# One attention stage, re-planned: merged value copies, a quarter of x moved by transfers, separate input loads

## The chip, the cores and the metric

The kernel runs on one core of a Trainium2 chip. The metric is the device time of the whole kernel in microseconds, the median of several runs. Engines are named as in the profile: PE is TensorE (matmuls), ACT is ScalarE, DVE is VectorE, POOL is GpSimd, SP is SyncE, which here only issues transfers.

## The reference

A gated linear attention over 4 batches, 8 heads, 768 steps and 48 features, and behind it a mixture of 8 experts whose gates are balanced over all tokens:

```python
f = 1.0 / (1.0 + np.exp(-f_logit))
for t in range(S):
    state = f[:, :, t, :, None] * state + np.einsum('bhd,bhe->bhde', k[:, :, t], v[:, :, t])
    y[:, :, t] = np.einsum('bhd,bhde->bhe', q[:, :, t], state)
...
logits = x @ w_gate                      # x: y as (3072, 384)
P = np.exp(logits - logits.max())
for _ in range(8):
    P /= P.sum(1, keepdims=True) + 1e-09
    P /= P.sum(0, keepdims=True) + 1e-09
    P *= N / E
for e in range(E):
    out += P[:, e:e + 1] * (np.maximum(x @ w1[e], 0.0) @ w2[e])
```

## The kernel before

Every number is kept as two 16-bit halves, a high and a low part, and a product is three matmuls. The high part is made by ScalarE (a copy with conversion), the low part by VectorE (value times scale minus high part).

The attention is cut into 24 items of 128 tokens (`attend(i)`). Three items are a unit `u` (384 tokens of a half batch), two units are a batch `b`. An item has streams of steps, each named by a letter: L loads its inputs; K makes the decayed keys (exponential, logarithm, a scan on VectorE, high and low keys, a transposing transfer); d the decays; Q the queries; V the values; A the scores; S the running states; c the carried state; Y the outputs, which end as the parts `xh` and `xl` of x; g the gates' logits. The first three items turn their keys on TensorE (T, U) instead of by transfers.

The output of an item lies in PSUM as four blocks of 96 rows. Three blocks go to rows 0 to 95 of x in one instruction; the fourth is cut into three pieces of 32 rows that go to rows 96 to 127, one instruction each (`PCS`, lines 642 and 648 by way of the helpers). So an item has four copies on ScalarE and four on VectorE. The values are rounded once to a compact high and low part (`vhc`, `vlc`) and written once more, for each of two heads and both parts, to block diagonal tiles (`vh`, `vl`): four copies of 64 x 384, for the first three items two of them by GpSimd.

While the attention runs, TensorE is filled with the first two experts' products over tokens that are ready ("filler", `raw_pairs`, streams named F; one F is one matmul). Filler results leave PSUM by evictions: E on ScalarE, D on VectorE. The second product of a filler pair is stored to memory (`put`, line 491) and added later. Filler uses a ring of four PSUM banks (`bank`). The gates' small product uses 16 spare columns of the bank of the keys-values product (`spare`, `kv_bank`).

The order in which every engine's instructions are issued is written out in `PLAN`: each word takes one step of a stream, `F3` takes three filler matmuls, `W25` 25 idle warm-up matmuls, `B` a step of the balancing of the gates (`balance`), `C0` to `C3` a step of `convert(b)`, which prepares the tokens of a batch for the paired products, `k0` to `k3` the preparation of the first weights. `X` stands behind the last gates: there the attention's memory is given back. All transfers named here are issued from SP's queue, in order.

Behind the plan comes the paired stage: for the other experts, products of blocks in a scheme that needs fewer multiplications (`period`, `paired`, tiles `kb_*`, `kyps`, `kxps`). It begins with one matmul into each of five PSUM banks (`kb_touch*`).

Of the kernel before, what the change touches and what calls it, by code (L numbers as in the profile page):

```python
# [9 lines left out]
F32 = mybir.dt.float32  # L10
# [9 lines left out]
NP = H // 2  # L20
# [34 lines left out]
A_IN_PSUM = range(3, 24)  # L55
LOW_BY_DVE = (0, 1, 2)
VL_BY_POOL = (0, 1, 2)
# [3 lines left out]
G L0 a0 a1 a2 a3 B a4 a5 a6 a7 L1 z G K0 W25 K0 Z K0 K0 Z Z Z K0 V0 K0 z a0 V0 K0 d0 K0 K0 V0 T0 K0 Q0 U0 W1 a0 T0 T0 U0 U0 W3 Q0 T0 b0 U0 L2 S0 Q0 c0  # L61
d0 V0 V0 S0 W3 Q0 a1 V0 c0 S0 A0 a1 S0 a2 W8 A0 a3 b1 S0 A0 S0 a2 a4 Y0 Y0 A0 a5 a3 Y0 a6 Y0 Y0 Y0 a4 Y0 Y0 Y0 a5 Y0 F1 b2 F1 K1 F6 K1 F2 Y0 F2 b3 a7
Y0 Y0 Y0 F1 K1 F1 K1 V1 g0 F5 b0 F9 g0 F1 a6 F2 d1 F1 K1 F10 E F3 K1 F6 Q1 F5 D F4 K1 F7 Q1 F3 K1 F4 K1 F1 E F1 L3 T1 U1 K1 Q1 F3 T1 D F1 Q1 F2 U1 F1
a7 F1 d1 T1 K2 F2 S1 A1 T1 K2 F1 V1 F2 V1 F2 V1 F1 A1 V1 S1 V2 K2 V1 F1 A1 F3 K2 b1 Y1 S1 A1 S1 Y1 E K2 U1 d2 K3 Y1 K2 U1 S1 V2 c1 S1 S1 Q2 S1 Y1 Y1
K2 c1 Y1 Q2 K2 K2 Y1 L4 T2 Y1 U2 K2 Y1 Y1 F2 Q2 Y1 F6 T2 T2 Q2 Y1 F3 Y1 F1 U2 Y1 F1 U2 b0 F1 T2 g1 F5 U2 F1 A2 d2 V2 S2 F2 g1 F2 V2 F1 A2 F1 S2 b2 V2
b1 c2 V2 A2 F6 b3 F3 S2 Y2 A2 F1 S2 F1 Y2 F1 E F9 K3 F6 Y2 K4 D F9 S2 F1 c2 F5 b2 F1 S2 F5 E F1 Y2 S2 Y2 V3 F1 D F1 K4 F3 S2 V4 F3 b3 F3 Y2 F1 K3 K3
F1 Y2 F2 Y2 F1 Y2 F1 Y2 F2 Y2 F1 K3 d3 F2 Y2 F4 Y2 E F4 Y2 F3 d3 K3 F2 Q3 F3 S3 F5 g2 V3 F1 K3 F9 K3 F3 K3 F3 g2 F1 K4 F3 E F9 V3 F7 K3 F1 V3 F7 V3 F8
V3 F5 D F3 E F8 V4 F1 K4 F2 K4 F1 K3 F1 d4 F6 D F1 V4 F7 d4 F1 K4 E F3 V4 F1 D F2 K4 F2 Q3 F1 K4 F1 K4 F2 L5 V4 F3 V4 F2 K4 F1 Q3 F4 Q3 S3 E F1 K4 F1
S3 S3 Q4 F2 S3 F3 A3 c3 S3 Q4 S4 S3 F5 A3 F2 Q4 L6 F9 S3 F2 A3 F6 S3 F3 K5 F3 A3 F2 E Y3 F1 Q4 F1 K5 Y3 F1 D V5 F1 Y3 F1 K5 K5 A4 Y3 F1 K6 F1 A4 d5 Y3
F1 Q5 F1 V5 Y3 F1 E F3 Q5 F4 Y3 F7 Y3 F3 Y3 F3 Y3 Y3 F3 A4 F5 Y3 F3 Q5 F1 Y3 F3 Y3 F2 A4 E F3 d5 g3 K5 D Y4 F2 V5 Y4 g3 K5 F1 V5 F1 Y4 Q5 S4 K5 F1 S4  # L70
S4 K5 K5 F1 S4 F2 V5 F2 E F2 K5 F1 V5 F1 c4 F1 S4 F3 S4 F1 S4 F4 S5 F1 E F1 K5 F2 L7 F3 K6 F2 S4 A5 V6 Y4 A5 F4 Y4 F3 K6 K6 F1 Y4 A5 F6 Y4 F7 Y4 F2 A5
F1 Y4 F2 d6 F2 E F6 V6 F2 Y4 F3 K6 F3 D F7 d6 F2 Q6 F2 Y4 F8 K7 F1 Y4 F3 Y4 F4 Y4 F1 E F2 K6 F7 V6 F3 g4 D Y5 K6 F4 Y5 g4 Q6 K6 F2 K6 F2 Y5 S5 V6 F2
# [91 lines left out]
DH = DM // 2  # L164
# [1319 lines left out]
```

## Time and profile before

| what | us |
|---|---|
| median of 3 runs | 1490.27 (1488.26 to 1490.68) |
| the profiled execution, its own time | 1490.65 |
| its span, first to last instruction | 1488.8 |
| TensorE, ScalarE, VectorE, GpSimd busy in it | 1444.7, 1167.7, 1274.0, 1060.1 |

The span leaves out 1.85 us around the instructions. Matmuls are pipelined and their ends are modelled, so a high busy time of TensorE alone doesn't show that it sets the pace; a count of matmuls times the beat at which they start does.

### The profile page before, as it was taken

To read this page: it belongs to the slowest core of one execution; us is meant where nothing else is said; L and a number is where in the kernel's file an instruction comes from. 1 tells how busy PE (TensorE), PEld (TensorE's weight loads), DVE (VectorE), ACT (ScalarE), POOL (GpSimd) and SP (SyncE) were. 2 spreads that over 40 slices of the span, in tenths; PEclk is the share of its full clock that TensorE was granted. 3 is DMA by queue.
4 is the path that set the end of the run, shared out by engine and by line. 5 is a ranking of instruction groups with operands and counts; after the bars stand their busy time and mean duration, and the time that the engine had idled before them with its cause. 6 is when DMAs were issued, how large, how long until landed. Compare 5 with 4: busy or idle time off the path is not lost.

```text
span 1488.8 us, 40831 instructions
## 1 busy us (share of the span) xinstructions
PE 1444.7 (97%) x16125; PEld 1276.8 (86%) x16125; DVE 1274.0 (86%) x2585; ACT 1167.7 (78%) x2636; POOL 1060.1 (71%) x1259
## 2 busy tenths in 40 slices
PE   7988999999999999999999999999999999999997
PEld 5777766666679999999999999999999999999997
DVE  7878979988869989999988888888888898888876
ACT  8888998874467788888888888887777777778764
POOL 3233443338436699999999999998888888888763
PEclk9999999999999999999999999999999999999999
DMA  8435545520200122221121111110000000000012
GB/s 261 112 102 131 136 116 142 126 48 33 77 31 12 29 61 60 56 60 49 49 60 50 40 53 50 55 49 23 23 23 23 22 23 20 15 13 23 2 55 78
DMA packets 82234, 88.97 MB, mean 60 GB/s; under 512 B 49808, under 2 KB 69392, under 8 KB 82032
## 3 DMA queue, kind: packets, MB, share of 16 engines
q1 hardware_dynamic: 81600, 85.68, 20.9%
q8 instruction: 128, 2.10, 0.6%
q14 instruction: 74, 0.61, 0.1%
q10 hardware_dynamic: 432, 0.59, 0.1%
HBM read 62.46 MB, written 14.16 MB: 51 GB/s over the span
## 4 chain that ended last, share of the span: by engine, by line
PE 78%; ACT 9%; DVE 7%; DMA 4%; issue 2%; SPq 0%; ACTq 0%; DVEq 0%
PE kyps L374 30%; PE kb_A L374 9%; PE kb_B L374 9%; PE kb_D L374 7%; PE kxps L374 5%; PE kb_C L374 5%; PE yps L374 4%; PE hps L374 4%; DMA q<-in_qkf_dram 3%; PE kb_E L374 2%; PE kb_F L374 2%; ACT xh L642 1%; DVE xl L648 1%; DVE sl L648 1%; ACT kb L642 1%
## 5 line engine op out<-in xcount | busy, mean ns | idle before, releaser
L374 PEld LDWEIGHTS <-k1h 128*128 128x128 f16 x3120 | 293.6, 98 | 22.0 <-issue 2.1
L374 PE MATMUL kyps<-k2h,kgh 128*128 128x192 f16 x1248 | 307.2, 246 | 1.5 <-ACT kyps L1189 1.5
L374 PE MATMUL kyps<-k2h,kgl 128*128 128x192 f16 x1248 | 307.4, 246 | 0.0
L374 PE MATMUL kyps<-k2l,kgh 128*128 128x192 f16 x1248 | 307.3, 246 | 0.0
L374 PEld LDWEIGHTS <-kgh 128*128 128x128 f16 x2496 | 229.8, 98 | 8.8 <-issue 1.8
L1359 POOL TENSOR_TENSOR kgl<-kf,kgh 128x512 f16<-128x512 f32 x153 | 204.2, 1335 | 4.4 <-ACT kgh L1356 4.4
L1192 DVE SCALAR_TENSOR_TENSOR yy<-kyps,pes,part 128x192 f32<-128x192 f32 x282 | 117.0, 415 | 102.4 <-PE kyps L374 92.2
L1231 POOL TENSOR_TENSOR acc<-acc,yy 128x384 f32<-128x384 f32 x141 | 141.0, 1000 | 67.0 <-DVE yy L1192 67.0
L1359 POOL TENSOR_TENSOR kgl<-kr,kgh 128x512 f16<-128x512 f32 x153 | 181.1, 1184 | 9.8 <-PE kyps L374 8.3
L374 PEld LDWEIGHTS <-k1l 128*128 128x128 f16 x1560 | 152.6, 98 | 17.7
L374 PEld LDWEIGHTS <-kh 128*128 128x128 f16 x1248 | 117.2, 98 | 8.7 <-issue 1.8
L374 PEld LDWEIGHTS <-kgl 128*128 128x128 f16 x1248 | 122.1, 98 | 0.1
L1189 ACT ACTIVATE kyps<-kyps 128x192 f32<-128x192 f32 x156 | 50.1, 321 | 73.4 <-PE kyps L374 71.3
L1336 POOL TENSOR_TENSOR kr<-kr 128x256 f32<-128x256 f32 x104 | 78.8, 758 | 38.8 <-ACT kr L1325 36.4
L1310 ACT ACTIVATE cp<-kb_A 128x512 f32<-128x512 f32 x156 | 93.3, 598 | 16.6 <-DVE kb_A L1312 15.5
L1356 ACT ACTIVATE kgh<-kf 128x512 f16<-128x512 f32 x156 | 98.6, 632 | 0.4 <-DVE kf L1333 0.4
L1356 ACT ACTIVATE kgh<-kr 128x512 f16<-128x512 f32 x156 | 97.9, 628 | 0.0
L645 POOL TENSOR_TENSOR kb<-q,kb 48x512 f16<-48x512 f32 x42 | 54.3, 1294 | 61.0 <-ACT kb L642 47.8
L374 PEld LDWEIGHTS <-w1h 128*128 128x128 f16 x1008 | 74.2, 100 | 24.1 <-issue 3.1
L374 PE MATMUL yps<-w2h,hh 128*128 128x384 f16 x288 | 94.7, 329 | 0.0
L374 PE MATMUL yps<-w2l,hh 128*128 128x384 f16 x288 | 94.7, 329 | 0.0
L374 PE MATMUL yps<-w2h,hl 128*128 128x384 f16 x288 | 94.6, 329 | 0.0
(285 smaller groups left out, 5484.1 us busy)
## 6 DMA issues: line engine op xcount, KB each, us to landing
q<-in_qkf_dram SPq DMA_DIRECT2D x23, 672.0 KB, 5.7
k1r<-in_w_dram SPq DMA_DIRECT2D x26, 384.0 KB, 3.0
k2r<-in_w_dram SPq DMA_DIRECT2D x26, 384.0 KB, 3.1
ys<-yr SPq DMA_DIRECT2D x48, 192.0 KB, 2.0
yb<-ys SPq DMA_DIRECT2D x48, 192.0 KB, 2.4
vr<-in_vbd_dram SPq DMA_DIRECT2D x24, 192.0 KB, 4.5
out_dram<-acc SPq DMA_DIRECT2D x21, 192.0 KB, 1.9
w1r<-in_w_dram SPq DMA_DIRECT2D x6, 384.0 KB, 7.2
```

The lines of the kernel that those rows point to most:

```text
L374: ins = (nc.tensor.transpose if transpose else nc.tensor.matmul)(**kw)
L642: pin(nc.scalar.activation(out=out, in_=in_, func=func, **kw))
L645: pin(eng.tensor_tensor(out=out, in0=in0, in1=in1, op=op))
L648: pin(nc.vector.scalar_tensor_tensor(out=out, in0=in0, scalar=scalar, in1=in1, op0=op0, op1=op1))
L1189: pin(nc.scalar.activation(out=out, in_=in_, func=AF.Copy, **kw))
L1192: pin(nc.vector.scalar_tensor_tensor(out=y, in0=ps, scalar=p, in1=z, op0=ALU.mult, op1=ALU.add))
L1231: pin(nc.gpsimd.tensor_tensor(out=y, in0=y, in1=z.rearrange("p s d -> p (s d)"), op=ALU.add))
L1310: pin(nc.scalar.activation(out=fresh(ev[2]), in_=bk, func=AF.Copy))
L1336: pin((nc.gpsimd if ev[2] == 'P' else nc.vector).tensor_tensor(out=r[:, 0], in0=r[:, 1], in1=r[:, 0], op=ALU.subtract))
L1356: pin(nc.scalar.activation(out=hs['g', t][0][i], in_=hs['f' if i else 'r', t], func=AF.Copy))
L1359: pin((nc.vector if tag == str(PERIODS - 1) else nc.gpsimd).tensor_tensor(out=hs['g', t][1][i], in0=hs['f' if i else 'r', t], in1=hs['g', ...
```

## The change

1. The plan is written anew: the same streams and the same number of filler matmuls in another order.
2. Units 3 to 6 (`X3_U`): the fourth block of the outputs is rounded in one instruction on each of ScalarE and VectorE into a tile of 96 rows, and when three items are done, six transfers bring it to rows 96 to 127 of x (stream x).
3. Values: both parts lie in one tile, and one copy for each head moves both, on ScalarE for all items.
4. Inputs: f, k, q and v are loaded by streams of their own (L, M, N, O), each with its own two buffers.
5. The scores of items 0 to 2 are masked in PSUM too, so VectorE makes their low part.
6. The gates use a bank of the filler's ring.
7. A store of an early output is issued behind the next eviction instead of at once.
8. The first tiles of the filler alternate between two experts; of the five touches two are moved into later slots; the last conversion has 40 slots instead of 15, in which it takes its remaining steps.

```diff
-A_IN_PSUM = range(3, 24)
+A_IN_PSUM = range(24)
-VL_BY_POOL = (0, 1, 2)
+V_BY_DVE = ()
+X3_U = (3, 4, 5, 6)
 PLAN = """
-G L0 a0 a1 a2 a3 B a4 a5 a6 a7 L1 z G K0 W25 K0 Z K0 K0 Z Z Z K0 V0 K0 z a0 V0 K0 d0 K0 K0 V0 T0 K0 Q0 U0 W1 a0 T0 T0 U0 U0 W3 Q0 T0 b0 U0 L2 S0 Q0 c0
...
+G N0 z O0 B M0 z L0 M1 O1 N1 a1 G W61 a3 a5 a6 V0 a0 V0 Z a4 Z a7 a2 Z L1 K0 O2 Z K0 V0 K0 K0 V1 V0 d0 V1 d0 O3 K0 a1 K0 Q0 L2 a1 K0 Q0 a3 b1 N2 Q0 a3
...
-CONVAT = (0, 1, 2, 3, 4, 5, 6, 7, 8, 9, 10, 11, 12, 13, 14)
+CONVAT = tuple(range(40))
+FIRST = ((0, 0), (1, 0), (0, 1), (1, 1), (0, 2), (1, 2))
...
     def evicted(name):
         while True:
+            held = stores.pop() if name == "E" and stores else None
             evictions[name].popleft()()
+            if held:
+                nc.sync.dma_start(out=held[0], in_=held[1])
             yield
...
-            nc.sync.dma_start(out=yscr[e][u, t * 128:(t + 1) * 128], in_=yr)
+            stores.append((yscr[e][u, t * 128:(t + 1) * 128], yr))
...
-        def loaded():
-            q3 = new("q3", [R, 3, L])
-            if i:
-                nc.sync.dma_start(out=q3, in_=qkf[i].rearrange("r n p t -> r n (p t)"))
+        def loaded(name, n):
+            nc.sync.dma_start(out=new(name, [R, L]), in_=qkf[i, :, n].rearrange("r p t -> r (p t)"))
+            yield
+
+        def loaded_v():
             nc.sync.dma_start(out=new("vr", [128, NB, D]), in_=vbd[i])
...
-            for t, rs in vh:
-                act(t, vr[rs], scale=VS)
-                yield
-            for t, rs in vl:
-                (pin(nc.gpsimd.tensor_copy(out=t, in_=vlc[rs])) if i in VL_BY_POOL else act(t, vlc[rs]))
+            for h in range(2):
+                rs = slice(64 * h, 64 * h + 64)
+                if i in V_BY_DVE:
+                    pin(nc.vector.tensor_copy(out=vv[rs, :, :, h, :], in_=vc[rs]))
+                else:
+                    act(vv[rs, :, :, h, :], vc[rs])
                 yield
...
+            parts = PCS[:1] if u in X3_U else PCS
+            if u in X3_U:
+                if not s % TT:
+                    thirds[u] = ap.tile([96, 2, HS], F16, name=f"x3_{u}", tag="x3", bufs=1)
+                x3 = [thirds[u][:, q, s % TT * TS:s % TT * TS + TS] for q in range(2)]
+                act(x3[0], yps[0:96, 3], scale=YS * XS)
+                yield
...
+            if u in X3_U:
+                three(x3[1], yps[0:96, 3], YS * XS, x3[0], ALU.mult, ALU.subtract)
+                yield
...
+        def moved():
+            for q, x in enumerate(xof(u)):
+                for n in range(3):
+                    nc.sync.dma_start(out=x[96:128, n, :], in_=thirds[u][32 * n:32 * n + 32, q, :])
+                ready.update((u, t, q, k) for t in range(TT) for k in range(KT))
                 yield
...
-            ps = spare[-1]
+            ps = bank([128, 2 * NE], f"lps_{i}")
...
-    for tag in ("A", "B", "D", "k1", "k2", "x"):
-        if tag != "A":
-            touched = pk.tile([128, 512], F32, name=f"kb_touch{tag}", tag=tag)
+    for tag, slot in (("x", 12), ("k2", 6), ("k1", 0), ("D", 0), ("B", 0)):
+        touched = pk.tile([128, 512], F32, name=f"kb_touch{tag}", tag=tag)
+
+        def touch(touched=touched):
             mm(out=touched, lhsT=ind[:, 0:128], rhs=ind[:, 0:512], start=True, stop=True)
+
+        if slot:
+            plan.setdefault((0, slot), []).append(touch)
+        else:
+            touch()
```

## Rows read from the trace of the kernel before

**Rows 1.** Busy time of each engine (instructions), granted clock, DMA share, by stretch.
```profile
core 0: us, PE busy (x) PEld busy (x) DVE busy (x) ACT busy (x) POOL busy (x), PEclk, DMA share, GB/s
25.00:340.40 315.40, 288.62 (x4199) 216.44 (x4197) 267.58 (x465) 272.73 (x597) 114.70 (x134) 0.98 0.47 116
340.40:418.50 78.10, 78.10 (x489) 47.74 (x488) 64.02 (x129) 32.97 (x69) 48.72 (x65) 1.00 0.18 57
...
440.00:1488.80 1048.80, 1038.84 (x11106) 985.85 (x11104) 910.08 (x1930) 824.93 (x1899) 882.51 (x1028) 1.00 0.13 38
```

**Rows 2.** Instructions on the gates' and balancing's tiles: duration min/median/max, first and last start.
```profile
L825 DVE TENSOR_REDUCE lg<-kvps x24: 143/166/175, 25.5 to 340.4; 128x8 f32<-128x16 f32 x24
...
L1003 DVE TENSOR_SCALAR pes<-pe x1: 259/259/259, 410.0 to 410.0; 128x192 f32<-128x192 f32 x1
```

**Rows 3.** Timeline of TensorE at the end of the filler: start, us, instruction.
```profile
404.00 0.33 PE L374 MATMUL yps<-w2h,hl 128*128 128x384 f16 x1
...
404.65 0.33 PE L374 MATMUL yps<-w2h,hh 128*128 128x384 f16 x1
...
418.32 0.38 PE L374 MATMUL kb_touchx<-ind 112*128 112x512 f16 x1
418.54 0.27 PE L374 MATMUL kb_A<-xbh,k1h 128*128 128x256 f16 x1
```

**Rows 4.** ScalarE's groups from 0 to 340.4: busy us, mean ns, idle before.
```profile
L642 ACT ACTIVATE vh<-vr 64x384 f16<-64x384 f32 x48 | 24.8, 517 | 0.5
L642 ACT ACTIVATE vl<-vlc 64x384 f16<-64x384 f16 x42 | 21.9, 521 | 0.8
...
L642 ACT ACTIVATE xh<-yps 32x128 f16<-32x128 f32 x72 | 19.1, 266 | 1.5
...
L490 ACT ACTIVATE yr<-yps 128x384 f32<-128x384 f32 x33 | 15.9, 482 | 1.8 <-PE yps L374 1.5
...
L642 ACT ACTIVATE q<-q 112x512 f32<-112x512 f32 x24 | 15.0, 626 | 13.4 <-DMA q<-in_qkf_dram 13.2
...
L984 ACT ACTIVATE xah<-xs 128x768 f16<-128x768 f32 x6 | 4.9, 834 | 0.0
...
L984 ACT ACTIVATE xbh<-xs 128x512 f16<-128x512 f32 x4 | 2.5, 628 | 0.0
...
L973 ACT ACTIVATE xbh<-xh 128x256 f16<-128x256 f16 x4 | 1.6, 412 | 0.0
```

**Rows 5.** VectorE's groups from 0 to 340.4, and one tile's spread (min/median/max).
```profile
L648 DVE SCALAR_TENSOR_TENSOR sl<-st,sh 48x384 f16<-48x384 f32 x40 | 29.8, 745 | 3.8 <-ACT sh L642 3.1
...
L648 DVE SCALAR_TENSOR_TENSOR xl<-yps,xh 32x128 f16<-32x128 f32 x72 | 20.6, 287 | 1.8
...
L485 DVE SCALAR_TENSOR_TENSOR hl<-hps,hh 128x384 f16<-128x384 f32 x32 | 17.7, 553 | 7.2 <-ACT hh L484 6.6
...
L645 DVE TENSOR_TENSOR al<-aps,ah 128x512 f16<-128x512 f32 x21 | 14.4, 685 | 2.4 <-ACT ah L642 2.3
...
L989 DVE TENSOR_TENSOR xal<-xs,xah 128x768 f16<-128x768 f32 x6 | 5.9, 979 | 0.1
L968 DVE TENSOR_REDUCE xmx<-x 128x1 f32<-128x768 f32 x6 | 5.7, 946 | 0.1
...
L989 DVE TENSOR_TENSOR xbl<-xs,xbh 128x512 f16<-128x512 f32 x4 | 2.6, 681 | 0.0
...
L648 DVE SCALAR_TENSOR_TENSOR sl<-st,sh x48: 341/555/2235, 17.9 to 335.7; 48x384 f16<-48x384 f32 x40, 48x192 f16<-48x192 f32 x8
```

**Rows 6.** Transfers (KB, us to landing), and the chain that ended last (start, us).
```profile
q<-in_qkf_dram SPq DMA_DIRECT2D x23, 672.0 KB, 5.7
...
q<-in_qkf_dram SPq DMA_DIRECT2D x3, 224.0 KB, 4.0
...
70.49 5.02 DMA q<-in_qkf_dram
...
238.61 6.87 DMA q<-in_qkf_dram
```

**Rows 7.** SP's own waits, 20 to 340 us: in total, times, longest.
```profile
SPq L491 <- ACT yr L490: 68.4, 16, 11.7
```

**Rows 8.** TensorE's waits, 20 to 320 us: in total, times, longest.
```profile
PE kvps L374 <- DVE lg L825: 5.3, 4, 2.2
```

**Rows 9.** Timeline of the start on ScalarE.
```profile
4.23 0.63 ACT L642 ACTIVATE q<-q 112x512 f32<-112x512 f32 x1 [0.30 <-DMA q<-in_qkf_dram]
21.02 1.05 ACT L642 ACTIVATE xh<-yps 96x384 f16<-96x384 f32 x3
```

More of the change, by code (lines that the diff above doesn't have):

```diff
@@ L465, in fast, with store @@
     tiles, planned = [0], [True]
-    evictions = {"E": deque(), "D": deque()}
+    evictions, stores = {"E": deque(), "D": deque()}, []
+    def store():
+        if stores:
+            to, yr = stores.pop()
+            nc.sync.dma_start(out=to, in_=yr)
     def evict(name, op):
@@ L600, in diagonal @@
         return [(v[rs, :, h, :], rs) for h, rs in ((h, slice(64 * h, 64 * h + rows.stop)) for h in range(2))]
-    vhs, vls = wide("vh", 128, NB, 96, 3), wide("vl", 128, NB, 96, 3)
+    vvs = [ap.tile([128, 2, NB * 96 + 32], F16, name=f"vv{i}", bufs=1) for i in range(3)]
+    nc.vector.memset(vvs[0][:, 0, :], 0.0)
+    nc.gpsimd.memset(vvs[0][:, 1, :].bitcast(I32), 0)
+    vhs, vls = ([t[:, n, :] for t in vvs] for n in range(2))
     shs, sls = wide("sh", R, NB, 96, 2), wide("sl", R, NB, 96, 2)
@@ L719, in values @@
             vr = o["vr"]
-            vhc, vlc = (new(f"v{v}c", [128, NB, D], F16) for v in "hl")
-            act(vhc, vr, scale=VS)
+            vc = new("vc", [128, 2, NB, D], F16)
+            o["vhc"], o["vlc"] = vc[:, 0], vc[:, 1]
+            act(vc[:, 0], vr, scale=VS)
             yield
-            three(vlc, vr, VS, vhc, ALU.mult, ALU.subtract)
+            three(vc[:, 1], vr, VS, vc[:, 0], ALU.mult, ALU.subtract)
             yield
-            for t, rs in vh:
-                act(t, vr[rs], scale=VS)
-                yield
-            for t, rs in vl:
-                (pin(nc.gpsimd.tensor_copy(out=t, in_=vlc[rs])) if i in VL_BY_POOL else act(t, vlc[rs]))
+            for h in range(2):
[4 more added lines that the diff above has]
+                    act(vv[rs, :, :, h, :], vc[rs])
                 yield
@@ L805, in outputs @@
                 yield
[L806 removed]
+            parts = PCS[:1] if u in X3_U else PCS
[5 more added lines that the diff above has]
+                yield
+            for n, (si, so) in enumerate(parts):
                 act(xh[so + (tok,)], yps[si], scale=YS * XS)
[L808 removed]
+                if u not in X3_U:
+                    ready.add((u, s % TT, 0, n - 1))
                 yield
[L810 removed]
+            if u in X3_U:
+                three(x3[1], yps[0:96, 3], YS * XS, x3[0], ALU.mult, ALU.subtract)
+                yield
+            for n, (si, so) in enumerate(parts):
                 three(xl[so + (tok,)], yps[si], YS * XS, xh[so + (tok,)], ALU.mult, ALU.subtract)
[L812 removed]
+                if u not in X3_U:
+                    ready.add((u, s % TT, 1, n - 1))
+                yield
+        def moved():
[3 more added lines that the diff above has]
+                ready.update((u, t, q, k) for t in range(TT) for k in range(KT))
                 yield
@@ L826, in gates @@
             yield
-        gens = dict(L=loaded, K=keys, d=decays, Q=queries, V=values, A=scores, S=states, c=carried, Y=outputs, g=gates)
+        gens = dict(L=lambda: loaded("f", 0), M=lambda: loaded("k", 2), N=lambda: loaded("q", 1), O=loaded_v, K=keys, d=decays, Q=queries, V=values, A=scores, S=states, c=carried, Y=outputs, g=gates)
+        if u in X3_U and s % TT == TT - 1:
+            gens["x"] = moved
         if by_pe:
@@ L925, in raw_pairs @@
     def raw_pairs(pairs):
-        todo = [(e, 0, t) for e in range(2) for t in range(TT)] + [(e, u, t) for u in range(1, TILED) for t in range(TT) for e in range(2)]
+        todo = [(e, 0, t) for e, t in FIRST] + [(e, u, t) for u in range(1, TILED) for t in range(TT) for e in range(2)]
         behind_ = []
@@ L931, in raw_pairs @@
             behind_.append((e, u, t, h))
-            while len(behind_) > (0 if e == u == 0 and t < TT - 1 or (e, u, t) == (1, 0, TT - 1) or u and e else 1):
+            while len(behind_) > (0 if not u and (e, t) != FIRST[-2] or u and e else 1):
                 yield from tile_down(*behind_.pop(0))
@@ L1140, in fast @@
     planned[0] = False
+    store()
     if next(filler, 0) or next(chain, chain) is not chain or any(next(gen, gen) is not gen for gen in converts[:3]) or not kept:
```

142 lines of the change are left out of this document (66 added, 76 removed).

## The prediction

> **What bounds the kernel now.** I read the kernel by stages first, because the shares of the whole span mix two programs. The table by stretch [rows 1] shows three. From 440 us to the end TensorE is busy 1038.84 of 1048.80 us: the paired stage is TensorE's, and nothing in the diff takes a matmul out of it. From 340.4 to 418.5 us TensorE is busy all 78.1 us, with ScalarE at 32.97 and VectorE at 64.02: these are the filler matmuls that were left when the attention ended. From 25 to 340.4 us, the attention, ScalarE is busy 272.73 and VectorE 267.58 of 315.4 us. TensorE's 288.62 there is no measure of a limit (its matmul records overlap). So the attention goes at the pace of ScalarE and VectorE together, and the filler is laid into TensorE's gaps.
>
> Two marks cut the stages. The last gates' reduction starts at 340.4 us, and the balancing is done at 410.0 [rows 2]; the first matmul of the paired stage starts at 418.54, right behind the touches [rows 3]. The balancing, 8.5 us early, is covered by filler. Between the marks TensorE streams 384-column matmuls at 0.1625 us each (404.00 to 404.65 for four steps) [rows 3].
>
> That gives the rule by which I cost everything: **end = end of the attention + filler left then + the fixed rest.** An edit that shortens the attention pays in full, as long as no filler is moved behind it. Counting the F words of the plan (one is one matmul), the plan before issues 1,877 of its 2,340 before the mark X behind the last gates and leaves 463; 463 x 0.1625 = 75.2 us, and the stretch took 78.1, so 2.9 us are other things.
>
> **The change, part by part.** *The plan.* The new plan issues 1,793 before X and leaves 547. All 84 moved ones are 384-column matmuls: 84 x 0.1625 = 13.65 us more behind the attention. This is the price of the change, and the attention has to end 13.65 us sooner for it to be even.
>
> *ScalarE in the attention.* x: the twelve items of units 3 to 6 copy the high part in two instructions instead of four. A 32x128 piece takes 0.266 us, and the new 96x128 one has the same columns: 12 x 2 x 0.266 = 6.4 us go [rows 4]. Values: 48 copies of 0.517 and 42 of 0.521 (46.7 us) become 48 of 768 columns. The trace has a 768-column copy at 0.834; by the slope between 128 columns (0.266) and 384 (0.517) it would be 0.893. I take 0.87: 41.8 us, so 4.9 go, with the six copies that were GpSimd's already in the new number. Evictions: the words E before X fall from 92 to 87, 5 x 0.482 = 2.4 us. The conversion of batch 1 stands at step 13 instead of 37 at X: 4 copies of 0.41, 3 of 0.834 and 2 of 0.628 move behind it, 5.4 us. Together 19.1 us [rows 4]. The moved ones land in the next stretch, where ScalarE has 45 us free [rows 1].
>
> *VectorE in the attention.* The low parts of x: 24 x 0.287 = 6.9 us go. Two evictions, 2 x 0.553 = 1.1. The conversion: 3 x 0.979 + 2 x 0.681 and one maximum of 0.946, 5.2. Against it, the scores of items 1 and 2 come from GpSimd, 2 x 0.685 = 1.4 more. Together 11.8 us less [rows 5]. The next stretch has 14.1 us free on VectorE and becomes 13.65 longer, so what moves there fits.
>
> The two engines take turns in one chain, so the work alone shortens the attention by something from 11.8 (VectorE decides) to 19.1 us (ScalarE decides). Neither stands out in [rows 1], so I take the middle, 15.5.
>
> *Inputs loaded separately.* Today one 672 KB transfer brings f, q and k of an item, 5.7 us to landing, into one of two buffers, so it can't be issued before the item two earlier has done with all three. ScalarE idles 13.4 us ahead of the first exponential of an item, 13.2 of it for this transfer [rows 4], and eight of these transfers lie on the chain that ended last, from 70.49 to 238.61 us, some 46 us of it [rows 6]. The three buffers come free one by one, and three 224 KB transfers landed in 4.0 us each at the start. Bounds: 0 back, if the pieces are as late as the whole; 13.4, if none is waited for. What ScalarE waits for next is its own partner, VectorE, so not all comes back: I take 8. The cost is two more issues an item on SP's queue, 46 in all at 0.33 to 0.44 us; SP has the room, but is in order.
>
> The Trainium skill speaks against this part: "DMA: Bandwidth & Descriptors", Anatomy of one DMA and Bandwidth, gives each transfer a fixed cost of about 2.0 us, measured on GpSimd's path, and asks for transfers of 1 MiB or more. By its fit one whole would be 3.5 us and three pieces 7.6 us one after the other, an estimate. The trace agrees that a third isn't a third of the time (4.0 against 5.7 us) [rows 6].
>
> *Stores.* An early output's store now waits behind the next eviction. SP stood 68.4 us behind ScalarE for such stores [rows 7], and what is queued behind them is transposes and loads. Its gain is part of the 8 us. *Transfers of x.* Six per unit, 24 in all, wait on SP for the low part of the third item; behind them stand loads and transposes. Their readers are the unit's gates, which the plan puts 19 to 36 filler matmuls later (over 3 us), and its filler, later still. Nothing in the trace moves from buffer to buffer this way; the nearest row is a store, so I bound it by 0 and by the 4.0 us of a third-size transfer once for each of four units, 16 us, and take 0 for the cover; without it the gates would stall TensorE, which has gaps.
>
> *Gates.* They leave the bank of the keys-values product, for whose reduction TensorE waited 5.3 us in four places [rows 8], and take a filler bank 24 times. TensorE shows no wait for an evicted filler bank in this stage, so the ring has room. Gain 0 to 5.3, cost 0 to 24 x 0.482 (an eviction's row) = 11.6; TensorE isn't the limit here, so 0 for both.
>
> *Start.* The plan loads q, v, k and then f of item 0, where f came first and its exponential ran at 4.23 us; first x at 21.02 [rows 9]. Three more transfers ahead at 0.43 us an issue, plus their bytes, put f some 2.5 us later. Value copies and zeroing now run in that hole, some 4 us of ScalarE's work that no longer lies later. Bounds: 0, and 5 us lost (the value copies ahead of it grow too). I take 1.5. FIRST alternates two experts over three tiles: same matmuls, 0. The touches at the stage's edge and the longer slots of the last conversion move at most two rows of 0.21 us; 0.
>
> **The sum**, against the profiled execution: its span is 1488.8, its time 1490.65, and the median of the runs is 1490.27, 0.4 below. Attention: 340.4 - 15.5 - 8 + 1.5 = 318.4. Filler behind it: + 13.65. So 22.0 - 13.65 = 8.4 us won: 1482.3, or 1482 as a median.
>
> "SBUF — State Buffer", Who interferes with whom, of the Trainium skill says that a VectorE instruction with two SBUF operands is shut out while GpSimd reads. The low part of the state agrees: 0.555 us in the median, 0.745 in the mean, 2.235 at most [rows 5]. By that rule taking GpSimd's sums and copies out of the attention would give VectorE some 2 us more, an estimate; the sum above leaves it out.
>
> **The rivals.** *A, the transfers stay late.* The pieces are issued in the same order on the same queue, behind the same waits, and nothing comes back: 15.5 - 1.5 - 13.65 = 0.35 us, 1490: no change. For it speaks that SP's long waits [rows 7] are for engines, not for buffers alone; against it, that a piece's buffer comes free earlier. The skill's fixed cost of a transfer would work this way.
>
> *B, slower: VectorE sets the pace.* Only its 11.8 us count, nothing comes back, because VectorE is what ScalarE would wait for, and the start loses its 5: 11.8 - 5 - 13.65 = -6.85, so 1497. It decides from the point where the attention ends later than 340.4 - 13.65 = 326.7 us. For it speaks VectorE's 267.58 of 315.4 beside ScalarE's 272.73; against it, that some of this is VectorE waiting inside instructions for GpSimd.
>
> *C, everything pays.* ScalarE's 19.1 and the whole 13.4, no loss at the start: 32.5 - 13.65 = 18.9, so 1472.
>
> **How the numbers follow.** The forecast 0.50, A 0.18, B 0.15, C 0.17. The likeliest one's own range is 1476 to 1488, from 12 us with half the other waits gone to none. The range from 1470 to 1492 takes in A and C and leaves out most of B. 0.2% is 3 us, about what a measurement tells from no change: faster than 1487.3 are the forecast (nearly all), C and a little of A, 0.71; within it most of A and a little of B, 0.16; slower the rest, 0.13.
>
> **What would show it.** The last gates' reduction at about 318 us, the first paired matmul some 91 us behind it (409 to 411), and the rest as long as before. ScalarE's idle time for input transfers down from 13.2 to about 5 us; ScalarE's busy time up to the last gates about 18 us less and VectorE's about 12. The gates should show no long wait for the moved quarter. The prediction is wrong if the last gates come later than 327 us, if TensorE pauses between them and the paired stage, because more conversion now has to fit there, or if the paired stage itself changes by more than 1 us.

## The result, and the profile after

The changed kernel takes 1470.13 us in the median (1467.46 to 1472.11, 4 runs) beside 1490.47 for the kernel before on the same chip: the ratio is 0.9865, 95% interval 0.9846 to 0.9884. The forecast was 1482 (1470 to 1492): the direction was right, the gain of 20 us was more than twice the 8.4 forecast, and the time lies at the very edge of the range. The profiled execution took 1470.28 us, its span is 1468.4.

The stretches first, in the columns of [rows 1]. The first row is the attention from 25 us to the last gates, the second the filler that is left, the third the paired stage.

```profile
25.00:306.30 281.30, 266.75 (x4146) 207.77 (x4145) 247.12 (x439) 251.66 (x523) 108.24 (x121) 0.98 0.54 131
306.30:397.40 91.10, 91.10 (x570) 55.66 (x569) 66.52 (x137) 39.18 (x83) 51.56 (x71) 1.00 0.17 53
440.00:1468.40 1028.40, 1018.82 (x10894) 966.98 (x10891) 893.51 (x1896) 809.47 (x1862) 872.88 (x1015) 1.00 0.13 39
```

The two marks [rows 2]: duration, first and last start of the gates' reductions and of the balancing's result.

```profile
L854 DVE TENSOR_REDUCE lg<-lps x24: 164/168/175, 29.5 to 306.3; 128x8 f32<-128x16 f32 x24
...
L1034 DVE TENSOR_SCALAR pes<-pe x1: 261/261/261, 357.8 to 357.8; 128x192 f32<-128x192 f32 x1
```

And the timeline of TensorE at the first paired matmul [rows 3], with one of the two touches that moved behind it.

```profile
397.44 0.27 PE L374 MATMUL kb_A<-xbh,k1h 128*128 128x256 f16 x1
...
403.42 0.38 PE L374 MATMUL kb_touchk<-ind 112*128 112x512 f16 x1
```

The last gates come 34.1 us earlier (306.3 against 340.4). The stretch behind them is 13.0 us longer (91.1 against 78.1). From the first paired matmul to the end it was 1488.8 - 418.54 = 1070.26 us and is 1468.4 - 397.44 = 1070.96, so 0.7 longer, with two touches inside. -34.1 + 13.0 + 0.7 = -20.4, the whole difference of the spans.

ScalarE up to the last gates, in the columns of [rows 4]:

```profile
L652 ACT ACTIVATE vv<-vc 64x768 f16<-64x768 f16 x48 | 39.9, 836 | 2.3 <-DVE vc L658 1.8
...
L652 ACT ACTIVATE f<-f 112x512 f32<-112x512 f32 x24 | 14.9, 623 | 0.2
...
L652 ACT ACTIVATE xh<-yps 32x128 f16<-32x128 f32 x36 | 9.6, 267 | 0.7
L652 ACT ACTIVATE x<-yps 96x128 f16<-96x128 f32 x12 | 3.1, 262 | 3.9 <-PE yps L374 3.9
```

The line to look at is the second: ahead of the first exponential of an item (it writes `f` now, `q` in [rows 4]) ScalarE stood idle for 13.4 us in all before, and for 0.2 now. VectorE [rows 5]:

```profile
L658 DVE SCALAR_TENSOR_TENSOR sl<-st,sh 48x384 f16<-48x384 f32 x40 | 25.6, 640 | 1.3 <-ACT sh L652 0.7
...
L658 DVE SCALAR_TENSOR_TENSOR xl<-yps,xh 32x128 f16<-32x128 f32 x36 | 10.3, 286 | 0.9
...
L658 DVE SCALAR_TENSOR_TENSOR x<-yps,x 96x128 f16<-96x128 f32 x12 | 3.4, 282 | 1.1 <-ACT xh L652 1.1
```

The inputs by thirds [rows 6], and the moved quarter of x: KB, us to landing.

```profile
q<-in_qkf_dram SPq DMA_DIRECT2D x24, 224.0 KB, 3.7
k<-in_qkf_dram SPq DMA_DIRECT2D x24, 224.0 KB, 4.0
f<-in_qkf_dram SPq DMA_DIRECT2D x24, 224.0 KB, 2.9
...
xh<-x SPq DMA_DIRECT2D x12, 24.0 KB, 2.3
xl<-x SPq DMA_DIRECT2D x12, 24.0 KB, 1.9
```

The chain that ended last, from 25 to 300 us, held eight input transfers of some 46 us before [rows 6]. Now its transfers are these three:

```profile
213.76 4.02 DMA k<-in_qkf_dram
253.04 1.81 DMA xl<-x
278.50 2.86 DMA xl<-x
```

TensorE's waits, 20 to 300 us [rows 8]: the wait for the gates' reduction is gone, and this small one for the moved quarter has come (0.2 us more are for `xh`).

```profile
PE lps L374 <- DMA xl<-x: 1.6, 4, 0.6
```

The start, on ScalarE [rows 9]: the exponential runs 3.5 us later and the first x 4.4 us later.

```profile
7.76 0.61 ACT L652 ACTIVATE f<-f 112x512 f32<-112x512 f32 x1
...
25.40 0.75 ACT L652 ACTIVATE xh<-yps 96x384 f16<-96x384 f32 x2
```

### The profile page after: what moved, and what is told of

It is laid out like the page before. It is cut to its first block, busy times and chain, and to the rows that moved or that the text cites. A ratio compares the mean times of both kernels' runs of the same rounds, so it can differ in the third digit from the quotient of the medians.

```text
span 1468.4 us, 40941 instructions
## 1 busy us (share of the span) xinstructions
PE 1438.4 (98%) x16146; PEld 1276.6 (87%) x16146; DVE 1255.1 (85%) x2563; ACT 1153.3 (79%) x2570; POOL 1056.6 (72%) x1251
## 3 DMA queue, kind: packets, MB, share of 16 engines
q1 hardware_dynamic: 88640, 86.27, 21.6%
## 4 chain that ended last, share of the span: by engine, by line
PE 79%; ACT 3%; DVE 3%; issue 1%; DMA 1%; SPq 0%; POOL 0%; DVEq 0%; ACTq 0%; POOLq 0%
PE kyps L374 31%; PE kb_A L374 9%; PE kb_B L374 9%; PE kb_D L374 7%; PE kxps L374 5%; PE yps L374 5%; PE kb_C L374 5%; PE hps L374 4%; PE kb_E L374 2%; PE kb_F L374 2%; ACT sh L652 0%; ACT vv L652 0%; ACT kb L652 0%; DMA xl<-x 0%; ACT f L652 0%
## 5 line engine op out<-in xcount | busy, mean ns | idle before, releaser
L655 POOL TENSOR_TENSOR kb<-k,kb 48x512 f16<-48x512 f32 x42 | 54.4, 1295 | 57.5 <-ACT kb L652 44.9
```

The source lines that it names most:

```text
L655: pin(eng.tensor_tensor(out=out, in0=in0, in1=in1, op=op))
```

## The experiments

Each kernel computes the whole reference. Differences are given to the median of the changed kernel (1470.1) or of the kernel before, which was 1490.4 to 1491.1 beside them; "the attention" is the start of the last gates' reduction. The changed kernel's own interval is 2.8 us either way and the others' 1 to 4, so a difference under some 3 us from it isn't clear of noise. The diffs leave out what only makes the rest fit.

### The plan without the lighter instructions, and they without the plan

The new plan with the separate loads, but with the old instructions: four copies of the values, four pieces of x in every unit, low scores of the first items by GpSimd.

```diff
-A_IN_PSUM = range(24)
+A_IN_PSUM = range(3, 24)
-                act(vv[rs, :, :, h, :], vc[rs])
+                act(vv[rs, 0, :, h, :], vr[rs], scale=VS)
...
+                act(vv[rs, 1, :, h, :], vc[rs, 1])
-                act(x3[0], yps[0:96, 3], scale=YS * XS)
+                for si, so in PCS[1:]:
+                    act(xh[so + (tok,)], yps[si], scale=YS * XS)
```

> The new plan with the old instructions: the fourth block of x in three pieces again (in the plan's same steps, no transfers of x), four value copies instead of two (the low part of the first three items by GpSimd), the low scores of items 1 and 2 by GpSimd. ScalarE gets back 24 x 0.267 = 6.4 us and 46.7 - 39.9 = 6.8 us. Theory W (ScalarE's work sets the attention's pace, one for one): 13 us slower than the changed kernel, about 1483. Theory P (the new order did it; the lighter instructions only fill time in which ScalarE would wait): within 4 us of it, 1470 to 1474. In between, each has its share.

Measured: 1489.33, ratio to before 0.9987 (0.9978 to 0.9996): 19.2 us more than the changed kernel and more than either theory allowed. The attention ends at 325.2, 15.2 us sooner than before, and the moved filler takes that back. ScalarE waits 0.4 us for f, k and q. From 25 us to there:

```profile
25.00:325.20 300.20, 269.70 (x4146) 207.27 (x4147) 256.74 (x462) 269.55 (x590) 111.98 (x126) 0.98 0.49 121
```

ScalarE is busy for nine tenths of it and VectorE for 86%: with the loads in time, the engines' work is what is left.

The old plan with all lighter instructions, whole loads, and a unit's moved quarter issued right ahead of its gates:

```diff
+X3_U = (3, 4, 5, 6)
-            tok = slice(s % TT * TS, s % TT * TS + TS)
+            todo = [i] if u not in X3_U else [3 * u + t for t in range(TT)] if s % TT == TT - 1 else []
```

> The kernel before, with its own plan, loads and stores, but the lighter instructions: values in two copies, the fourth block of units 3 to 6 by one instruction and transfers (a unit's three gates then together), all scores masked in PSUM. No filler is moved, so nothing is paid. Theory W: 13 us faster than before, 1477. Theory P: at most 4 us faster, 1486 to 1490, with ScalarE's idle time grown by what its work lost.

Measured: 1504.02, 1.0094 (1.0079 to 1.0108), slower where both theories said faster. TensorE's waits, 20 to 350 us, show the moved quarter without cover:

```profile
PE kvps L375 <- DMA xh<-x: 10.8, 6, 4.9
...
PE kvps L375 <- DMA xl<-x: 2.6, 6, 0.5
```

So the cover was put back: the same kernel, with a unit's three gates run where the first gates of the next unit stand.

```diff
-            todo = [i] if u not in X3_U else [3 * u + t for t in range(TT)] if s % TT == TT - 1 else []
+            todo = [] if u in X3_U else [i]
+            if u - 1 in X3_U and not s % TT:
+                todo = [i - 3, i - 2, i - 1] + todo
```

> The kernel before with all the lighter instructions, as in the run that came out 13 us slower, but the gates of units 3 to 6 run with the next item's, so that the six transfers have a whole item's work to land in. If the uncovered transfers cost those us (TensorE waited 13.4 us for them) the loss goes and the lighter instructions show: some 1475 to 1480. If the old order itself can't use them: 1490 or slower.

Measured: 1492.11, 1.0016 (1.0004 to 1.0028). The cover is worth 11.9 us, and the lighter instructions are worth nothing in the old plan. Its profile names what holds them: ScalarE's wait for the inputs has grown from 12.9 to 17.8 us (20 to 340 us), and of the chain's eight input transfers six are left, 35.7 us, the first and the last of them here.

```profile
ACT q L646 <- DMA q<-in_qkf_dram: 17.8, 11, 3.1
```

```profile
70.24 5.04 DMA q<-in_qkf_dram
...
237.18 6.76 DMA q<-in_qkf_dram
```

At that point two theories stood: an order written for the old durations can't use lighter instructions, or the whole loads hold them. The last kernel of this line loads f, k and q separately in the old plan: f by a word of its own (`F2 d7 m9 F2`) behind the sixth step of the keys of the item two before, k and q where the whole load stood.

```diff
-                nc.sync.dma_start(out=q3, in_=qkf[i].rearrange("r n p t -> r n (p t)"))
+            for n, name in ((0, "f"), (2, "k"), (1, "q")):
+                if n or i < 2:
+                    nc.sync.dma_start(out=new(name, [R, L]), in_=qkf[i, :, n].rearrange("r p t -> r (p t)"))
+        def loaded_f():
+            nc.sync.dma_start(out=new("f", [R, L]), in_=qkf[i, :, 0].rearrange("r p t -> r (p t)"))
```

> The old plan with all lighter instructions and covered transfers of x (1492.1 us, ScalarE waiting 17.8 us for inputs), and f, k and q loaded separately as well: f of an item as soon as the decays of the item two before are used, k and q where the whole load stood. Theory 1, the old order of all engines' instructions, made for the old durations, holds the attention: the last gates at 332 to 340 us and a time of 1487 to 1493, though ScalarE's wait for inputs falls below 5 us. Theory 2, the input loads are what keeps the lighter instructions from paying in the old order: the wait comes back as time, the last gates at 322 to 328 us, 1475 to 1481.

Measured: 1472.82, 0.9882 (0.9867 to 0.9897), 19.3 us less than with whole loads and 2.7 more than the changed kernel, with overlapping intervals. The theory of the order, which had been mine, falls. In the profile the gates' last reduction, the attention's row and the exponential:

```profile
L800 DVE TENSOR_REDUCE lg<-kvps x24: 158/165/175, 25.3 to 322.4; 128x8 f32<-128x16 f32 x24
```

```profile
25.00:322.40 297.40, 280.42 (x4197) 212.60 (x4196) 263.60 (x443) 257.80 (x531) 108.96 (x128) 0.99 0.49 126
```

```profile
L586 ACT ACTIVATE f<-f 112x512 f32<-112x512 f32 x24 | 14.9, 622 | 0.4 <-DMA f<-in_qkf_dram 0.2
```

VectorE and ScalarE are as busy as with whole loads (261.26 and 258.84 there), in 16.6 us less. All the filler is still in this attention, so its end at 322.4 pays in full.

The old plan with the merged value copies alone was run as well.

```diff
+                act(vv[rs, :, :, h, :], vc[rs])
```

> The kernel before with only the values in two copies instead of four (the low part of the first three items by ScalarE as well). If the lighter instructions are worth the same in the old order: 3 us faster than before, 1487.5. If the old order can't use them, 1490 or slower.

Measured: 1494.88, 1.0027 (1.0015 to 1.0038): 4.3 us slower, with 13.7 us of waits for whole loads (20 to 340 us, where the kernel before has 12.9). One row is new there:

```profile
ACT vv L645 <- DVE vc L651: 6.9, 7, 1.7
```

The merged copy reads both parts, so it stands behind VectorE's low part; before, the copies of the high part read the input alone and the row is absent. ScalarE's copies take 40.3 us instead of 46.7, and this wait takes back the 6.4 saved. In the changed kernel it is 1.8 us. It is no bar in the old plan once the loads are separate, for it is 7.8 us there too (1472.82). Why this kernel comes out slower, and not even, stays open.

### What the lighter instructions are worth in the new plan

Four pieces of x in units 3 to 6 and no transfers of x, the rest as changed:

```diff
-                act(x3[0], yps[0:96, 3], scale=YS * XS)
+                for si, so in PCS[1:]:
+                    act(xh[so + (tok,)], yps[si], scale=YS * XS)
```

> The changed kernel with only the fourth block of x in three pieces again. Theory W: 24 x 0.267 = 6.4 us more, 1476.5. Theory P: 0 to 2 us. If the transfers of x had been a wait of their own, the kernel could even get faster.

Measured: 1483.22, 0.9951 (0.9936 to 0.9965): 13.1 us lost, twice what theory W said, the attention at 318.6. Four copies of the values (the values' part of the first diff above):

> The changed kernel with only the values in four copies again. Theory W: 6.8 us more, 1477. Theory P: 0 to 2 us.

Measured: 1473.19, 0.9885 (0.987 to 0.9901): 3.1 us lost, hardly clear of noise. The low scores of items 0 to 2 back on GpSimd (`A_IN_PSUM = range(3, 24)`):

> The changed kernel with only the scores of items 0 to 2 masked in SBUF again, the low part of items 1 and 2 by GpSimd. VectorE loses 1.4 us. The old instructions together cost 19.2 us, the pieces 13.1 and the copies 3.1; if the three add up, this is the rest, 3 us slower; by VectorE's time alone it would be 1 us faster.

Measured: 1471.43, 0.987 (0.9854 to 0.9887): 1.3 us, no more than the measurement tells. One by one they give 17.5, together 19.2.

Which engine's part of the 13.1 is it? One kernel cuts only ScalarE's instruction into three, one only VectorE's; the transfers stay.

```diff
-                act(x3[0], yps[0:96, 3], scale=YS * XS)
+                for n in range(3):
+                    act(x3[0][32 * n:32 * n + 32], yps[32 * n:32 * n + 32, 3], scale=YS * XS)
```

> The changed kernel, transfers of x and all, but the high part of the fourth block goes into the 96-row tile by three ScalarE instructions of 32 rows instead of one: 24 x 0.267 = 6.4 us more on ScalarE, all else as it is. Theory M (the stage takes the longer of the two engines, as the forecast's middle assumed): 1 to 6 us slower. Theory S (the two engines wait for each other in turn, so that what each loses adds up): 6.4 us slower, 1476.5, and the next kernel's loss comes on top. Theory T (the twelve pieces were costly for another reason, such as the transfers' cover or the PSUM bank): within 1 us.

```diff
-                three(x3[1], yps[0:96, 3], YS * XS, x3[0], ALU.mult, ALU.subtract)
+                for n in range(3):
+                    ns = slice(32 * n, 32 * n + 32)
+                    three(x3[1][ns], yps[ns, 3], YS * XS, x3[0][ns], ALU.mult, ALU.subtract)
```

> The changed kernel with the low part of the fourth block by three VectorE instructions instead of one: 24 x 0.287 = 6.9 us more on VectorE. Theory M: 0 to 2 us slower, since ScalarE is the busier (272 of 306 us against 262). Theory S: 6.9 us slower, 1477, so that this and the kernel with ScalarE's pieces together give the 13.1 us of all pieces. Theory T: within 1 us.

Measured: 1476.93, 0.9902 (0.9886 to 0.9917), and 1476.51, 0.9903 (0.9888 to 0.9917): 6.8 and 6.4 us lost, by 24 instructions of 0.266 (6.4 us) and of 0.287 (6.9) [rows 4, 5]. Each engine's work is paid nearly in full, and within the intervals the two add up to the 13.1. Then 24 small copies of ScalarE for which nobody waits:

```diff
+                if u in X3_U:
+                    for _ in range(2):
+                        act(idle, identh[0:32, :])
```

> The changed kernel with two extra ScalarE copies of 32x128 into an unused tile in each of the twelve items, behind the high part: the same 24 instructions, but nothing waits for them. If it is ScalarE's time that counts: 6 us slower, as with the three pieces. If it is the delay in the item's own chain (VectorE waits for the pieces): within 2 us.

Measured: 1474.29, 0.9884 (0.9868 to 0.99): 4.2 us. These copies aren't the same instructions as the pieces, as the expectation took them to be: they last longer.

```profile
L653 ACT ACTIVATE idle<-identh x24: 292/308/311, 155.0 to 281.2; 32x128 f16<-32x128 f16 x24
```

So 4.2 of some 7.4 us are paid, where 6.8 were paid for 6.4 of pieces that VectorE waits for. ScalarE's time alone costs; that the place in the chain adds to it is likely, but the two intervals overlap and don't settle its size. All value copies moved from ScalarE to VectorE (`V_BY_DVE = range(24)`):

> The changed kernel with all the merged value copies on VectorE instead of ScalarE: ScalarE loses 48 x 0.836 = 40 us, VectorE gets 48 copies of 768 16-bit columns, which no row prices yet; a VectorE instruction of 384 to 512 columns takes 0.55 to 0.69 us, so by that 40 to 50 us. Theory S or M: by those prices within 10 us of the changed kernel, faster only if the copy costs VectorE under some 0.5 us. The Trainium skill (VectorE: DVE Perf Modes) gives 16-bit copies a faster mode; by it they would cost far less and the kernel gain until TensorE, which is 90% full in this stage by its matmuls' beat, sets the end.

Measured: 1480.89, 0.9934 (0.9921 to 0.9947): 10.8 us lost. The copy on VectorE, and ScalarE's largest wait from 20 to 320 us:

```profile
L737 DVE COPY vv<-vc x48: 323/357/1229, 8.4 to 302.7; 64x768 f16<-64x768 f16 x48
```

```profile
ACT sh L652 <- DVE st L655: 20.9, 16, 2.9
```

One copy takes 0.357 us where ScalarE needs 0.836, and still the exchange loses: up to the last gates ScalarE is busy 36 us less and VectorE 18 us more, and ScalarE spends much of its freed time waiting for VectorE: the 20.9 us above were 1.0 in the changed kernel.

### The loads

The new plan, with f, k and q in one transfer at the place of the last of the three words; 16 steps of the keys that stood ahead of it follow it.

```diff
-            nc.sync.dma_start(out=new(name, [R, L]), in_=qkf[i, :, n].rearrange("r p t -> r (p t)"))
+            nc.sync.dma_start(out=q3, in_=qkf[i].rearrange("r n p t -> r n (p t)"))
```

> The changed kernel with f, k and q of an item in one 672 KB transfer again, issued where the last of its three words stands (the keys' steps of an item that stood ahead of that word, 16 in all, move right behind it). If the separate loads are worth what the forecast took (8 us, up to 13.4): 5 to 13 us slower, with ScalarE waiting for the transfer again. If the order of SP's queue and not the cut was what made the transfers late: within 2 us.

Measured: 1551.83, 1.0412 (1.0398 to 1.0426): 82 us lost, where 13 at most were expected. ScalarE's wait for inputs is 66.1 us in 17 places. Two timelines, of SP and of ScalarE, show one of them:

```profile
153.89 1.30 SPq L638 DMA_TRANSPOSE kt<-kb  x1
155.28 0.53 SPq L604 DMA_DIRECT2D q<-in_qkf_dram  x1
```

```profile
161.21 0.63 ACT L594 ACTIVATE q<-q 112x512 f32<-112x512 f32 x1 [4.84 <-DMA q<-in_qkf_dram]
```

To tell the size of the transfer from its place, three separate loads were written at that same late place, and one whole load at the early place (with three buffers, which fit only beside four pieces of x).

```diff
-Y4 F2 N9 F3 E F5
+Y4 F2 F3 E F5
...
-F1 K7 L9 F2 D F1
+F1 K7 F2 D F1
...
-F2 Y5 M9 Q8 E F7
+F2 Y5 L9 M9 N9 Q8 E F7
```

> The changed kernel, with the three loads of an item (224 KB each) issued one behind the other at the place of the last of them; the keys' steps that stood ahead of that place follow it. It is the kernel with whole loads, but for the size of the transfers. Theory 1, the place is what counts (separate buffers let the logits of the decays come early, and the whole could not): within some 15 us of the whole loads' 1551.8, so 1535 to 1555, ScalarE waiting 50 to 70 us for inputs. Theory 2, the size is what counts (a third lands in 2.9 to 4.0 us and the first exponential needs only the first third, where the whole took 5.5): 17 waits shorter by 2 to 3 us, so some 40 us less, 1500 to 1520.

```diff
-Y4 F2 N9 F3 E F5
+Y4 F2 L9 F3 E F5
...
+            q3 = new("q3", [R, 3, L], bufs=3)
+            nc.sync.dma_start(out=q3, in_=qkf[i].rearrange("r n p t -> r n (p t)"))
```

> The changed kernel with four pieces of x (1483.2 us), and f, q and k of an item in one 672 KB load again, at the place of the first of the three separate ones, which three buffers instead of two allow. Theory 1, the place is what counts: 1481 to 1486, no wait of ScalarE for inputs. Theory 2, the size is what counts: the whole lands 2 us later than a third and holds the queue for longer, so waits of 1 to 3 us in ten places or more come back, 1488 to 1500.

Measured: 1474.85, 0.9891 (0.9876 to 0.9906), 4.7 us lost; and 1485.71, 0.9969 (0.9959 to 0.998), 2.5 more than four pieces of x alone, with overlapping intervals. Neither theory holds for both: thirds at the late place cost little, and so does a whole in good time, though it still lands in 5.8 us (ScalarE waits 4.7 us for it, in three places). The timelines of the late thirds say why, SP's first:

```profile
144.88 0.33 SPq L603 DMA_DIRECT2D f<-in_qkf_dram  x1
146.95 0.33 SPq L603 DMA_DIRECT2D q<-in_qkf_dram  x1
...
156.85 0.43 SPq L603 DMA_DIRECT2D k<-in_qkf_dram  x1
```

```profile
156.93 0.63 ACT L594 ACTIVATE f<-f 112x512 f32<-112x512 f32 x1
```

Written side by side, the three aren't issued side by side: f of item 12 goes out at 144.88, 12 us ahead of its exponential, and k only at 156.85, when that exponential starts. In the changed kernel, where the words stand apart, the same three go out in the same order:

```profile
138.80 0.33 SPq L661 DMA_DIRECT2D f<-in_qkf_dram  x1
140.87 0.33 SPq L661 DMA_DIRECT2D q<-in_qkf_dram  x1
...
150.99 0.43 SPq L661 DMA_DIRECT2D k<-in_qkf_dram  x1
```

So moving the words left the order as it was. The loads' place on SP's queue follows when their buffers come free, not the plan's words, which the prediction took for SP's order. A third waits for its own buffer. In the trace of the late thirds VectorE's product of keys and decays, the last to read item 10's f, starts at 144.18 and takes 0.68 us; its last reading of that item's q starts at 146.23 and takes 0.69; each load goes out when it ends. GpSimd's last reading of that item's k starts at 151.07 and takes 2.89, and k follows behind the transposing transfer and one of v. The whole waits for the last of the three: its issue above stands right behind the transposing transfer of the item two before, which waits for that same work of GpSimd. What SP waits for ahead of its loads shows it in sum, for the late thirds (20 to 320 us) and the late whole (20 to 340):

```profile
SPq L603 <- DVE k L600: 35.3, 13, 5.0
```

```profile
SPq L604 <- POOL kb L597: 13.3, 6, 7.7
```

With a third buffer the whole is in time too; that kernel changes buffer and place at once, so the two aren't told apart there, but the late thirds show that the written place alone is not it.

### The moved filler, the stores and the gates

84 filler matmuls, with five evictions of ScalarE and two of VectorE, put back ahead of X in the new plan, spread from the states of item 12 on, so that 463 are left behind X:

```diff
-S12 Y11 E F4 A12 F2 x11 F2 Q13 F7 D F2 A12 F8 S12
+S12 Y11 E F5 A12 F2 x11 F2 Q13 F6 D F5 A12 F9 S12
```

> The changed kernel with 84 filler matmuls (13.65 us) moved back before X: from item 12's states on, filler and evictions run some 15% denser, in their own order, the rest of the plan unchanged. The forecast called these 13.65 us the price of the change. If that holds and TensorE's gaps take them, the attention ends when it did or 2.4 us later (five evictions) and the kernel is about 11 us faster, 1459. Rival: the filler and its evictions take the attention's time, so that it ends some 13 us later and nothing is won, 1470; then the moved filler was no price, and part of the attention's shortening was only deferral.

Measured: 1469.98, 0.9861 (0.9838 to 0.9884): no change. But the attention ends 11.2 us later:

```profile
L796 DVE TENSOR_REDUCE lg<-lps x24: 161/173/176, 29.8 to 317.5; 128x8 f32<-128x16 f32 x24
```

Behind it, the first paired matmul starts at 398.33, so that the filler left takes 80.8 us instead of 91.1. What the 84 matmuls and their evictions cost behind X, 10.3 us here, they cost ahead of it as well, 11.2. Stores issued at once again, and the gates back in the bank of the keys-values product:

```diff
-            stores.append((yscr[e][u, t * 128:(t + 1) * 128], yr))
+            nc.sync.dma_start(out=yscr[e][u, t * 128:(t + 1) * 128], in_=yr)
```

> The changed kernel with each early output's store issued at once, as before. If the stores held SP's queue up, and with it loads and transposes: 2 to 8 us slower, and SP's wait for ScalarE at the stores back from 47 to some 68 us. If not: within 1 us.

```diff
-            ps = bank([128, 2 * NE], f"lps_{i}")
+            ps = t[:, CT * NP * D + 2 * NE * at_:CT * NP * D + 2 * NE * (at_ + 1)]
```

> The changed kernel with the gates' product back in spare columns of the bank of the keys-values product (three sets of 16, since a unit's gates now come together). The forecast gave this part 0. Rival: the next item's product waits for the gates' reduction again, up to 5 us slower; or the filler's ring was hurt by it, up to 5 us faster.

Measured: 1471.03, 0.9872 (0.9849 to 0.9895), and 1469.06, 0.9857 (0.9834 to 0.988): neither part does anything that can be told.

## Why the prediction was right in direction and wrong in size

**The frame held.** End = attention + filler left + fixed rest: the three differences make up the 20.4 us of the spans, and the fixed rest moved by 0.7. The 13.65 forecast for the filler behind X was 13.0.

The range held by 0.1 us, and that is luck: its lower end was drawn to take in rival C, whose sum came near the time for another reason (below). The forecast's own range, 1476 to 1488, missed.

**First failing step: "Neither stands out, so I take the middle, 15.5."** That ScalarE and VectorE take turns in one chain was read as a price between the two engines' sums. The runs show that both are paid: pieces of x 6.8 on ScalarE and 6.4 on VectorE, 13.1 with both. The prediction's counts for the lighter instructions, 6.4 + 4.9 on ScalarE and 6.9 - 1.4 on VectorE, have 8.4 as their middle and 16.8 as their sum; measured in the new plan they are worth 19.2. Value copies alone gave 3.1 for the 4.9 counted, though one costs 0.836 and not the 0.87 taken, which would make the count 6.6; so not every microsecond is paid. Nor is adding up a rule for any exchange: the copies moved from ScalarE to VectorE gained 36 us on one and cost 18 on the other, and lost 10.8; in this plan a microsecond of VectorE counted for more than one of ScalarE.

**Second: "not all comes back: I take 8."** The wait for inputs fell from 13.2 to nothing. And its worth isn't bounded by those 13.4: once the instructions are lighter, the old plan's wait is 17.8 and taking it away gives 19.3 us. The bound was read from a trace with the heavier instructions; that their work hid part of the lateness is the likely reason. The reason given ahead of the change, that a third's buffer comes free earlier, is what SP's timelines of the late thirds and the late whole show.

**Third, and behind both: the terms were added as if each stood alone.** Lighter instructions with covered transfers but whole loads: 1492.1, 1.5 us more than before. Separate loads and the new plan with the old instructions: 1489.3, 1.8 less than the kernel before beside it. Both together: 1470.1 in the new plan, 1472.8 in the old one. Either edit takes away one of two limits that lie close together and leaves the other, so each alone shows nothing, and each looks like the whole gain when it comes last. (Separate loads in the old plan with the old instructions weren't run; the new plan stands in for them.) The plan's own order and the rest of the change, given both, are worth 2.7 us, no more than the intervals allow for noise.

**Fourth: "84 x 0.1625 = 13.65 us more behind the attention. This is the price of the change".** It was paid behind X, but it bought 11.2 us ahead of X, a term that the prediction put at nothing: the filler back in place changes the end by nothing. The prediction took TensorE's gaps for free. In the changed kernel they are few (TensorE is busy 266.75 of 281.30 us from 25 us on, by records whose ends are modelled), and the seven evictions take time of the two engines; which of the two makes the 11.2 was not separated.

Taken one after the other, the 34.1 us by which the attention got shorter come out like this: 11.2 for the moved filler (forecast: 0), 18.9 for the lighter instructions on top of everything else (325.2 to 306.3; forecast: 8.4), and so 4.0 for loads, deferred conversion, evictions and start with the old instructions (forecast: 13.6 of the 22.0). The split holds for this order alone, and it takes the filler's 11.2 from a kernel with the lighter instructions.

**What was right.** The moved quarter costs next to nothing with the gates behind cover (TensorE waits 1.8 us for it; a count of the plan gives 17 to 37 filler matmuls between, not 19 to 36), and 11.9 us without it, inside the bound of 16. The gates' bank is 0, as taken. The start lost more than the 1.5 taken, 4.4 at the first x, inside the bound of 5. The deferred conversion fits in its new stretch: TensorE is busy all 91.1 us. Of the marks that the prediction gave, ScalarE's wait for inputs went to nothing where about 5 was said; ScalarE is busy 21.8 us less up to the last gates (294.02 and 272.25) where 18 was said, and VectorE 21.6 less (283.94 and 262.34) where 12 was.

Of the 9.8 us that VectorE has over its count, the low part of the state gives 4.2: 40 x (0.745 - 0.640), with the same median of 0.555. The Trainium skill, "SBUF — State Buffer", Who interferes with whom, says that a VectorE instruction with two SBUF inputs contends with a GpSimd instruction that reads SBUF; the prediction put some 2 us on it, without a working, and left them out. Whether the trace agrees is open: these rows have less over their median, and GpSimd is busy 108.24 us instead of 114.70, but that is 38.5% of the shorter stretch where it was 36.4% of the longer. No run separated it.

"DMA: Bandwidth & Descriptors", Anatomy of one DMA, of the Trainium skill was the page that spoke against separate loads. The trace doesn't agree for this use: the thirds land in 2.9, 4.0 and 3.7 us each, they overlap (an f and a q went out at 102.36 and 102.82), and from 20 us to the last gates VectorE's 0.4 us for one k is the only wait of ScalarE or VectorE for them. Its Rules for kernel authors also say to issue early and wait late, and the runs agree with that: a whole in time lost 2.5 us, not clear of noise, a late one 82.

**Rivals.** A and B are out. C, everything pays, gave 1472 and was nearest, with 32.5 us of attention against 34.1 measured, though it reached that with ScalarE's sum alone rather than both engines' together.

## What to carry to other kernels

When two limits lie close together (an in-place buffer whose reload comes late, and two engines that feed each other), cost the pair: take the wait away on paper first, then ask what the instructions are worth, because either alone shows nothing. Where two engines hand work to each other many times, price a saving on both by a run that changes one engine's instructions alone instead of taking a middle, and treat idle slots as free only until the stage gets shorter. Before combining transfers, ask which buffers the combined one must wait for; that mattered here by tens of microseconds, its size by two or three at most.

## What the runs showed of the hardware that was not expected

- Three transfers of 224 KB instead of one of 672 KB cost nothing that can be seen: 2.9 to 4.0 us to landing each, against 5.7.
- A 64x768 16-bit copy from SBUF to SBUF takes 0.357 us on VectorE in the median (up to 1.229) and 0.836 on ScalarE.
- A 32x128 copy on ScalarE takes 0.308 us from SBUF (16 bits) in the median, and a piece of the same shape 0.266 from PSUM.
- Transfers of 24 KB from one SBUF tile to another land in 1.9 to 2.3 us; without work behind them TensorE waited up to 4.9 us for one.
